# Transformer block, forward and backward: three quarters of dW2 computed behind the attention forward and summed in DRAM, the rest alternating with dW1

## The chip, the cores and the metric

The kernel runs on one core of a Trainium2 chip. It computes the output of a transformer block and all gradients in one launch. The metric is the device time of one execution in microseconds; less is better. The kernel before has a median of 2522.99 us in three runs (2513.47 to 2525.77).

## The reference

One sequence of 2048 tokens, width 512, 32 heads of 16, an MLP of width 1792, bf16. The six modulation vectors come from `silu(c) @ w_mod`. Cut to what matters here:

```python
def _B_ref(x, w1, b1, w2, b2):
    h = jnp.einsum('bsd,df->bsf', x, w1) + b1
    r = jnp.where(h > 0, h, 0)
    h = r * r
    return jnp.einsum('bsf,fd->bsd', h, w2) + b2
...
h = _layernorm(x) * (1 + ca) + sa
x = x + ga * _A_ref(h, A_wqkv, A_wo)        # attention over 32 heads
h = _layernorm(x) * (1 + cb) + sb
x = x + gb * _B_ref(h, B_w1, B_b1, B_w2, B_b2)
...
_out, _vjp = jax.vjp(_f, A_x, A_wqkv, A_wo, B_w1, B_b1, B_w2, B_b2, c, w_mod)
_grads = _vjp(grad_out)
```

The change concerns dW2, the gradient of `B_w2`: with a = r * r (1792 features by 2048 tokens) it is gb times a @ grad_out, a sum over all tokens. The sums dgb (dW2 times w2, over features) and the gradients of b2 and of the columns 3, 4 and 5 of w_mod hang on the same products. dW1 is the like sum of xhat and du over the tokens.

## The kernel before

**Stages.** Tokens come in four chunks of 512 (SC = 4), features in 14 blocks of 128 (FT), heads in 8 groups of 4 (NQ), keys in 16 blocks of 128 (ST). First come the projections together with the attention of chunk 0. Then `fwd_rest` runs the attention of chunks 1 to 3: 3 x 8 x 16 = 384 units, one per chunk, head group and key block. A unit is four score products (L503), two exps on ScalarE (L507) and sixteen small products of P and V (L482). `last_chunk` then does the MLP and its backward for chunk 3 with no attention beside it, and the weight gradients dW1 (`gen_dw1`) and dW2 (`gen_dw2`) over all four chunks: the dW stage. The attention backward follows, then a last stage of projections.

**Background.** The MLP, forward and backward, of chunks 0 to 2 is written as generators (`gen_mlp`) that yield after each matrix product. Each unit of `fwd_rest` calls `bg.burst(3.0, self, most)`, which runs generators in the order in which they were added until its credit is spent, at most 4 products (5 or 2 in the first units of a group). Where it runs fewer, the unit adds products of the same size that nobody reads (L520, the filler). A tuple such as `("wait", 9)` is a marker: the background holds, and each unit takes 2 off. Other tuples mark places that the code can run up to (`until`).

**What a chunk's background holds.** When a chunk's last group is done, `take_o` copies its attention output, stores it to DRAM twice (`O_d`, L1264, in bf16 and L1266 in fp32) and `gen_mlp` starts. SyncE transposes the output (L1277) and grad_out (L1279) by DMA. Then follow the output projection and layernorm, fc1 with the relu (L1316, into `rT`), the backward through fc2 (L1326, into `auT`), the storing of both in DRAM (`duT_d`, `aT_d`), the backward through fc1 with a layernorm backward and the gradient of the attention output per 128 tokens (`gen_do`, which loads O_d by POOL at L1398), and fc2 for the four blocks of 128 tokens. Three of these four fc2 blocks come after the marker `fc2_2` in chunk 2, and `last_chunk` works them off at its start (`bg.take`, `bg.drain`).

**The dW stage.** `gen_dw1` takes one block of 128 features at a time: 64 products (L1096, 16 blocks of tokens by 4 of columns), one fp32 product that spreads db1 (`csb`, L1101), and per column tile three DVE operations (L1110, L1112, L1115) that form the block of dW1 and two sums. `gen_dw2` takes 16 products (L1151) per block, then two DVE operations (L1154, L1157) and a sum on POOL (L1158). Both need their features with tokens on partitions: `turned` loads per block 12 tiles by DMA transpose from DRAM (`tm_blk`, L1047) and, for the last chunk, four blocks at a time from SBUF (`tm_l`, L1051). dW2 begins when dW1's last block is under way. The columns 3 and 4 of the gradient of w_mod (L1170 to L1182) lie inside dW2, after its blocks 2 and 5. What the backward needs first is loaded in pieces between dW2's later blocks.

**What sets the order.** PE and SyncE work in the order of the program text; POOL, DVE and ACT in an order that the compiler's scheduler sets. The background has one PSUM bank (`pps`).

Of the kernel before, what the change touches and what calls it, by code (L numbers as in the profile page):

```python
# [112 lines left out]

class Pools:
# [12 lines left out]
class K:  # L127
# [32 lines left out]

    def build(self, ctx: ExitStack):
# [20 lines left out]
        self.WmT_d = self.dram("WmT_d", [DT, P, 3 * DT * P], BF16)  # L182
        self.dx1b_d = self.dram("dx1b_d", [512, D], BF16)
# [108 lines left out]
    def phase_fwd(self):  # L292
# [29 lines left out]
        QTm = [fw.tile([P, 512], BF16, name=f"QTm{j}") for j in range(4)]  # L322
# [139 lines left out]
    def fwd_rest(self, bg, KT, kp, pup, QTm, Vaug, O32):  # L462
# [33 lines left out]
        for n, (qc, g) in enumerate(groups):  # L496
            for kb in range(ST):
# [14 lines left out]
                done = 0 if qc == SC - 1 and f"fc2_{SC - 2}" in bg.seen else bg.burst(3.0, self, most)  # L512
# [348 lines left out]
    def last_chunk(self, bg, O_b, x0s, o32):  # L861
# [12 lines left out]
        tps = self.open_pool("tps", bufs=2, space=PSUM)  # L874
# [15 lines left out]
        g_tm = e0.tile([P, ST, D], BF16, name="g_tm")  # L890
        xh2 = e0.tile([P, ST, D], BF16, name="xh2")
        gt4, xh = g_tm[:, st0:, :], xh2[:, st0:, :]
        OT, gT = self.OT_l, self.gT_l
        nc.sync.dma_start(gt4, tm_v(io["grad_out"][0]))
        nc.sync.dma_start(xh2[:, :st0, :], self.xhat2_d.rearrange("(st p) d -> p st d", p=P)[:, :st0, :])
        nc.sync.dma_start(g_tm[:, :st0, :], io["grad_out"][0].rearrange("(st p) d -> p st d", p=P)[:, :st0, :])
# [56 lines left out]
        fill.add(self.gen_dw1(w1p, xh2, duT))  # L953
# [63 lines left out]
        fill.add(g2)  # L1017
# [9 lines left out]
        fill.until("dw1")  # L1027
        next(g2)
        self.open_bwd()
# [10 lines left out]
    def turned(self):  # L1040
# [4 lines left out]
        def get(pool, src, src_d, ft):  # L1045
            r = pool.tile([P, ST - 4, P], BF16, name="tm_blk", bufs=4)
            nc.sync.dma_start_transpose(r[:], src_d[ft, :, :(ST - 4) * P])  # L1047
            if ft % 4 == 0:
                n = min(4, FT - ft)
                t = pool.tile([P, 4, 4, P], BF16, name="tm_l", bufs=2)  # L1050
# [3 lines left out]
            return [r[:, st, :] for st in range(ST - 4)] + [lasts[-1][:, ft % 4, i, :] for i in range(4)]  # L1054
# [3 lines left out]
    def gen_dw1(self, sb, xh2, duT):  # L1058
# [6 lines left out]
        dsb_part = sb.tile([P, DT, FT], F32, name="dsb_part", bufs=1)  # L1065
        db1_row = sb.tile([P, 4 * P], BF16, name="db1_row", bufs=1)
# [18 lines left out]
        for ft in range(FT):  # L1085
# [4 lines left out]
            else:  # L1090
                yield ("dw1", 0)
            du, (w1_blk, diag) = dus[ft], blks[ft]
            g4 = self.dps.tile([P, DT, P], F32, name="dps")
            for kt in range(DT):
                for st in range(ST):
                    nc.tensor.matmul(g4[:, kt, :], lhsT=xh2[:, st, kt * P:(kt + 1) * P], rhs=du[st],  # L1096
                                     start=(st == 0), stop=(st == ST - 1))
                    if st % 4 == 3:
                        yield 1
            csb_ps = self.mps.tile([P, 512], F32, name="pps")  # L1100
# [6 lines left out]
            dw1 = sb.tile([P, DT, P], BF16, name="dw1")  # L1107
            for kt in range(DT):
# [5 lines left out]
                junk2 = sb.tile([P, P], BF16, name="junk", bufs=1)  # L1114
                nc.vector.scalar_tensor_tensor(junk2[:], csb[:], 1.0, w1_blk[:, kt, :], ALU.mult, ALU.mult,  # L1115
                                               accum_out=dsb_part[:, kt, ft:ft + 1])
            with nc.allow_non_contiguous_dma(reason="256B runs"):
                nc.gpsimd.dma_start(dw1_v[:, :, ft * P:(ft + 1) * P], dw1[:])
        for r in range(0, FT, 4):
# [3 lines left out]
        nc.vector.tensor_reduce(self.dsb_col[:], dsb_part[:], axis=AX.X, op=ALU.add)  # L1123

    def gen_dw2(self, sb, g_tm, aT, tb):
# [8 lines left out]
        def load(ft):  # L1134
            r = turned(tb, aT, self.aT_d, ft)
            w = sb.tile([P, D], BF16, name="w2_blk", bufs=3)
            nc.gpsimd.dma_start(w[:], io["B_w2"][ft * P:(ft + 1) * P, :])
            blks.append((r, w))

        mods = {2: (3, self.dsb_col), 5: (4, self.dcb_col)}  # L1140
# [4 lines left out]
        for ft in range(FT):  # L1145
            if ft + 3 < FT:
                load(ft + 3)
            a, w2_blk = blks[ft]
            pt = self.dps.tile([P, 512], F32, name="dps")
            for st in range(ST):  # L1150
                nc.tensor.matmul(pt[:], lhsT=a[st], rhs=g_tm[:, st, :], start=(st == 0), stop=(st == ST - 1))  # L1151
# [916 lines left out]
```

## Time and profile before

The profiled execution took 2527.3 us, with a span of 2525.3 us from the first instruction to the last.

| stage | from to, us | us |
|---|---|---|
| attention of chunks 1 to 3, with background | about 280 to 984 | 704 |
| start of the last chunk, up to fc1 | 984 to 1008.5 | 24.5 |
| MLP of the last chunk | 1008.5 to 1060 | 51.5 |
| dW1, with what is left of the last chunk | 1060 to 1124 | 64 |
| dW2 | 1124 to 1179.4 | 55.4 |
| backward and last stage | 1179.4 to the end | 1346 |

A row of a group of instructions reads: line, engine, operation, output and inputs, their shapes, the number of instructions, then busy microseconds and the mean of one in ns, then the idle time of the engine just before them and what ended it. A row of the timeline begins with start and length in microseconds. PE is the matrix engine, PEld its weight loads, DVE, ACT, POOL and SP the vector, scalar, GpSimd and sync engines. A row with SPq is the time that SP's queue spent issuing. Consecutive products overlap, so three or four of them have a combined length larger than the step from start to start.

### The profile page before, as it was taken

Reading aid. Unit: us, or ns where it says so; the run is one execution under the profiler, and the core shown is the slowest. Engines: PE = TensorE matmul, PEld = TensorE weight load, DVE = VectorE, ACT = ScalarE, POOL = GpSimd, SP = SyncE. Lnnn points to the kernel's source line nnn. Section 1 sums busy time; section 2 is a strip of 40 time slices with the busy share of each in tenths; the row PEclk is TensorE's granted clock in tenths of the full one; section 3 lists DMA queues with packets and bytes.
Section 4 is the critical chain, followed back from the end, with each engine's and each line's share of the span. In section 5 each row is a group of like instructions: output and inputs, shape, how many; then the busy total and the mean of one; then the engine's idle time right before and its main releaser. Section 6 shows DMA issues by size and latency. Waiting matters only on the chain.

```text
span 2525.3 us, 69141 instructions
## 1 busy us (share of the span) xinstructions
PE 2424.0 (96%) x26994; PEld 1032.7 (41%) x27199; DVE 1683.0 (67%) x3343; ACT 2283.0 (90%) x3757; POOL 715.7 (28%) x1265
## 2 busy tenths in 40 slices
PE   8999999999999999989999999999999999999988
PEld 4555444545554544573232333332333333333333
DVE  6222212322342333576999999999999999999857
ACT  7999999999999996533999999999999999999934
POOL 2344430120121021246222332322332323222323
PEclk9999999999999999999999999999999999999999
DMA  4689650451244054599999999999999999999997
GB/s 166 133 179 209 162 124 22 127 118 48 99 103 100 22 145 120 111 188 214 236 237 226 233 237 232 236 226 228 230 233 234 233 234 234 239 227 238 241 179 188
DMA packets 1291630, 454.19 MB, mean 180 GB/s; under 512 B 1235796, under 2 KB 1260246, under 8 KB 1291302
## 3 DMA queue, kind: packets, MB, share of 16 engines
q1 hardware_dynamic: 1252422, 344.68, 72.4%
q0 software_dynamic: 36800, 104.04, 14.1%
q8 instruction: 212, 3.47, 0.6%
q10 hardware_dynamic: 2080, 1.05, 0.2%
q14 instruction: 116, 0.95, 0.1%
HBM read 75.83 MB, written 64.49 MB: 56 GB/s over the span
## 4 chain that ended last, share of the span: by engine, by line
PE 40%; ACT 8%; DMA 8%; issue 2%; DVE 2%; POOL 0%; SPq 0%; DVEq 0%; ACTq 0%; POOLq 0%
PE st L1710 16%; PE acckv L1561 8%; ACT pu L1713 6%; PE accq L1586 5%; DMA dsT<-ds 4%; PE dps L1151 2%; PE dp L1624 2%; DMA keep<-ds 1%; DMA dqT<-dq_t 1%; ACT csq L1642 1%; PE st L1856 1%; DVE ds L1628 1%; PE dp L1761 1%; PE st L1667 1%; PE st L1574 1%
## 5 line engine op out<-in xcount | busy, mean ns | idle before, releaser
L1628 DVE TENSOR_TENSOR ds<-dp,pu 128x512 bf16<-128x512 f32 x1888 | 1166.8, 684 | 36.5 <-PE dp L1624 20.6
L1713 ACT ACTIVATE pu<-st 128x512 bf16<-128x512 f32 x2048 | 1073.6, 666 | 37.2 <-PE st L1710 21.3
L507 ACT ACTIVATE pu<-st 128x1024 bf16<-128x1024 f32 x768 | 704.9, 1127 | 6.0 <-PE st L503 5.6
L1624 PE MATMUL dp<-kvm,q 64*128 64x512 bf16 x1024 | 364.0, 383 | 2.1 <-DVE ds L1628 1.0
L1624 PE MATMUL dp<-kvm,dOTg 64*128 64x512 bf16 x1024 | 364.9, 384 | 1.0 <-DVE ds L1628 0.8
L1710 PE MATMUL st<-kvm,QTg 64*128 64x512 bf16 x1024 | 348.8, 382 | 6.0
L1710 PE MATMUL st<-kvm,q 64*128 64x512 bf16 x1024 | 347.9, 381 | 5.1 <-ACT pu L1713 0.2
L1643 POOL TENSOR_TENSOR ds<-csq,pu 128x512 bf16<-128x512 f32 x128 | 147.2, 1150 | 626.5 <-ACT csq L1642 547.4
L482 PEld LDWEIGHTS <-pu 128*128 128x128 bf16 x6144 | 216.5, 96 | 158.0 <-issue 83.2
L482 PE MATMUL accbank<-Vaug,pu 128*128 128x17 bf16 x6144 | 265.2, 172 | 10.1 <-ACT pu L507 7.4
L520 PE MATMUL st<-QTm,KTq 128*128 128x512 bf16 x670 | 202.7, 379 | 6.3 <-ACT pu L507 2.7
L413 ACT ACTIVATE pu<-st 128x1024 bf16<-128x1024 f32 x224 | 206.6, 1060 | 2.3 <-PE st L410 1.9
L503 PE MATMUL st<-QTm,KTq 32*128 32x512 bf16 x1536 | 171.9, 385 | 5.2 <-issue 1.0
L1561 PE MATMUL acckv<-ds,Qg 128*16 128x512 bf16 x1024 | 176.5, 383 | 0.2
L1561 PE MATMUL acckv<-pu,dOg 128*16 128x512 bf16 x1024 | 176.4, 383 | 0.0
L1561 PE MATMUL acckv<-ds,q 128*16 128x512 bf16 x1024 | 175.8, 382 | 0.0
L1561 PE MATMUL acckv<-pu,q 128*16 128x512 bf16 x1024 | 175.8, 382 | 0.0
L410 PE MATMUL st<-QTm,KTq 128*128 128x512 bf16 x435 | 130.0, 377 | 10.1 <-ACT pu L413 4.0
L1710 PEld LDWEIGHTS <-q 64*128 64x128 bf16 x1024 | 66.9, 94 | 162.9 <-issue 150.0
L1710 PEld LDWEIGHTS <-QTg 64*128 64x128 bf16 x1024 | 67.1, 94 | 161.5 <-issue 146.5
L347 PEld LDWEIGHTS <-pu 128*128 128x128 bf16 x2048 | 86.4, 96 | 59.6 <-issue 3.0
L1624 PEld LDWEIGHTS <-q 64*128 64x128 bf16 x1024 | 88.8, 93 | 51.3 <-issue 40.8
(399 smaller groups left out, 3365.7 us busy)
## 6 DMA issues: line engine op xcount, KB each, us to landing
KTq<-KTq_d POOLq DMA_DIRECT2D x24, 512.0 KB, 3.8
duT_d<-auT POOLq DMA_DIRECT2D x3, 1792.0 KB, 7.3
aT_d<-rT POOLq DMA_DIRECT2D x3, 1792.0 KB, 11.9
KTq_d<-KTq SPq DMA_DIRECT2D x32, 128.0 KB, 2.2
QTq_d<-ev_fm SPq DMA_DIRECT2D x32, 128.0 KB, 4.4
ktm_d<-ev_tm POOLq DMA_DIRECT2D x32, 128.0 KB, 2.6
VTq_d<-vT POOLq DMA_DIRECT2D x4, 1024.0 KB, 6.1
dx<-dx_d SPq DMA_DIRECT2D x16, 256.0 KB, 4.6
```

What stands on the lines that cost most here:

```text
L410: nc.tensor.matmul(stt[:, a, :], lhsT=KT[:, kb * P:(kb + 1) * P], rhs=QTm[2 * jp + a][:], start=True, stop=True)
L413: nc.scalar.activation(pu[:], stt[:], ACT.Exp, scale=self.scale)
L482: nc.tensor.matmul(acc[:, j, sub, :], lhsT=pus[half][:, a, sub * P:(sub + 1) * P], rhs=Vaug[:, kb, 4 * g + j, :], start=(kb == 0 and j == ...
L503: nc.tensor.matmul(tiles[h // 2][:, h % 2, :], lhsT=KT[r, kb * P:(kb + 1) * P], rhs=QTm[g % 2][r, :], start=True, stop=True)
L507: nc.scalar.activation(pu[:], t[:], ACT.Exp, scale=self.scale)
L520: nc.tensor.matmul(tiles[0][:, 0, :], lhsT=KT[:, 0:P], rhs=QTm[g % 2][:], start=True, stop=True)
L1561: nc.tensor.matmul(acckv[r:r + DH, :], lhsT=T[n][:, ib, col:col + DH], rhs=src[:, a, :], start=(ib == 0), stop=(ib == ST - 1))
L1624: nc.tensor.matmul(dp[:], lhsT=T["dOT"][rd, ib * P:(ib + 1) * P], rhs=masked["VT"][a][rd, 512 * c:512 * (c + 1)], start=True, stop=True)
L1628: nc.vector.tensor_tensor(dsg[:, i, a], dp[:], pu[:, a, :], ALU.mult)
L1643: nc.gpsimd.tensor_tensor(dsg[:, i, 1], f[:], pu[:, 1, :], ALU.mult)
L1710: nc.tensor.matmul(stt[:], lhsT=T["QT"][rs, q], rhs=masked["KT"][a][rs, c0:c0 + 512], start=True, stop=True)
L1713: nc.scalar.activation(pu[:, a, :], stt[:], ACT.Exp, scale=self.scale)
```

## The change

**dW2 of chunks 0 to 2 as background.** A new generator, `gen_early`, computes per block of 128 features the four products of one chunk (180 in all, with a 15th block of ones for db2) and leaves an fp32 sum of 128 x 512 in DRAM, `dw2p_d`. Chunk 0 stores its products; chunks 1 and 2 load the sum so far, add and store. The transposed features are read back from `aT_d` by DMA, two blocks ahead, into three buffers; the sums have four, in the space of `auT`. The blocks of chunks 0 and 1 are computed in the background of the next chunk, 0 to 6 ahead of the output projection and 7 to 14 in place of a marker; chunk 2's between its own fc2 blocks 1 and 2. Only fc2's block 3 is left behind the marker `fc2_2`. The burst's rate goes from 3.0 to 4.0.

**dW stage.** `gen_dw2` computes the last chunk only, four products per block instead of 16, and adds the loaded fp32 sum (three DVE operations per block). `weave` alternates its blocks with those of dW1 from dW1's fourth block on. From then on dW1's sum over csb times w1 is no longer taken by DVE: four PE transposes, an ACT copy and a product (`add_rows`) do it. The columns 3 and 4 of w_mod's gradient come after dW1's last block.

```diff
-                done = 0 if ... else bg.burst(3.0, self, most)
+                done = 0 if ... else bg.burst(4.0, self, most)
...
-        yield ("wait", 9 if sc else 14)
+        if sc:
+            self.open_early(sc - 1)
+            yield ("wait", 12)
+            yield from self.gen_early(sc - 1, 0, FT // 2)
+        else:
+            yield ("wait", 14)
...
-            yield ("wait", 11)
+            yield from self.gen_early(sc - 1, FT // 2, FT + 1)
...
+        if sc == SC - 2:
+            self.open_early(sc)
         yield from fc2(0)
         yield from self.gen_do(sc, *todo.pop(0))
+        yield from fc2(1)
+        if sc == SC - 2:
+            yield from self.gen_early(sc, 0, FT + 1)
+        yield from fc2(2)
         yield (f"fc2_{sc}", 0)
-        for k in range(1, 4):
-            yield from fc2(k)
+        yield from fc2(3)
...
+    def load_early(self, c, ft):
+        if ft < self.FT:
+            nc.sync.dma_start_transpose(self.dw_blk[ft % 3], self.aT_d[ft, :, 512 * c:512 * (c + 1)])
+        if c:
+            nc.sync.dma_start(self.dw_sum[ft % 4], self.dw2p_d[ft])
...
+    def gen_early(self, c, a, b):
+        for ft in range(a, b):
+            if ft + 2 <= FT:
+                self.load_early(c, ft + 2)
+            pt = self.mps.tile([P, 512], F32, name="pps")
+            for st in range(4):
+                lhs = self.dw_blk[ft % 3][:, st, :] if ft < FT else self.ones_b[:]
+                self.mm(pt[:], lhsT=lhs, rhs=self.dw_op[:, st, :], start=(st == 0), stop=(st == 3))
+                yield 1
+            s = self.dw_sum[ft % 4]
+            if c:
+                nc.vector.tensor_tensor(s, pt[:], s, ALU.add)
+            else:
+                nc.vector.tensor_copy(s, pt[:])
+            nc.gpsimd.dma_start(self.dw2p_d[ft], s)
```

```diff
         next(g2)
+        fill.gens = [weave(g1, g2)]
+        fill.until("bwd")
         self.open_bwd()
...
+            if ft >= F0:
+                ...
+                for kt in range(DT):
+                    nc.tensor.transpose(tp[:, kt, :], w1_blk[:, kt, :], self.ident[:])
+                turnedw[ft] = sb.tile([P, D], BF16, name="w1T", bufs=2)
+                nc.scalar.copy(turnedw[ft][:], tp[:].rearrange("p a b -> p (a b)"))
+                if ft > F0:
+                    add_rows(ft - 1)
...
-            for st in range(ST):
-                nc.tensor.matmul(pt[:], lhsT=a[st], rhs=g_tm[:, st, :], start=(st == 0), stop=(st == ST - 1))
+            for st in range(4):
+                nc.tensor.matmul(pt[:], lhsT=a[st], rhs=g_tm[:, st, :], start=(st == 0), stop=(st == 3))
                 yield 1
-            dw2 = sb.tile([P, D], BF16, name="dw2")
-            nc.vector.tensor_tensor(dw2[:], pt[:], self.mod_row(5), ALU.mult)
...
+                nc.vector.tensor_tensor(part[:], pt[:], part[:], ALU.add)
+                dw2 = sb.tile([P, D], BF16, name="dw2")
+                nc.vector.tensor_tensor(dw2[:], part[:], self.mod_row(5), ALU.mult)
+                nc.gpsimd.dma_start(io["out_6"][ft * P:(ft + 1) * P, :], dw2[:])
+                nc.vector.tensor_tensor(part[:], part[:], w2_blk[:], ALU.mult)
+                nc.gpsimd.tensor_tensor(dgb[:], dgb[:], part[:], ALU.add)
```

**SP, opening of the last chunk's attention.** First the kernel before, then the kernel with the change. `fT` holds the transposed attention output and grad_out, `QTm_143`, `QTm_144` and `auT` the early operands.

```order
192 L1434 DMA_TRANSPOSE dOTq<-dOpad_4895 128x8x128
193 L1277 DMA_TRANSPOSE fT<-O_b 128x16x128
194 L1279 DMA_TRANSPOSE fT<-in_grad_out_dram 128x4x512
195 L1302 DMA_TRANSPOSE fT<-xh_14265 128x16x128
196 L1343 DMA dx_d<-dx_16110 128x512
```

```order
207 L1560 DMA_TRANSPOSE dOTq<-dOpad_4896 128x8x128
208 L1355 DMA_TRANSPOSE fT<-O_b 128x16x128
209 L1357 DMA_TRANSPOSE fT<-in_grad_out_dram 128x4x512
210 L1467 DMA auT<-in_grad_out_dram 128x4x512
211 L1475 DMA_TRANSPOSE QTm_143<-aT_d 128x4x128
212 L1477 DMA auT<-dw2p_d 128x512
213 L1475 DMA_TRANSPOSE QTm_144<-aT_d 128x4x128
214 L1477 DMA auT<-dw2p_d 128x512
215 L1475 DMA_TRANSPOSE auT<-aT_d 128x4x128
216 L1477 DMA auT<-dw2p_d 128x512
```

The early operands, and a sum per block, come into SP's order behind the two large transposes.

**ACT, from the last blocks of dW1 to the backward.** Before, then with the change. `csb` and `t` belong to dW1, `O_20016` and `O_20348` are scratch of the modulation columns (diagonal, then the row), and `pu<-st` is the backward's first exp.

```order
117 L1170 ACTIVATE O_20016<-ident_f,dcb_col 128x128
118 L1170 ACTIVATE O_20016<-ident_f,dsb_col 128x128 x4
119 L1170 ACTIVATE O_20016<-ident_f,dcb_col 128x128 x3
120 L1175 COPY O_20016<-dps 128x512
121 L1179 ACTIVATE auT<-O_20016,scT 128x512 x4
122 L1175 COPY O_20016<-dps 128x512
123 L1179 ACTIVATE auT<-O_20016,scT 128x512 x4
124 L1713 ACTIVATE pu<-st 128x512 x6
```

```order
130 L1154 ACTIVATE t_20295<-csb,modT 128x128 x4
131 L1167 COPY dsb_rows<-tp 32x512
132 L1208 ACTIVATE O_20348<-ident_f,dcb_col 128x128 x4
133 L1217 COPY O_20348<-dps 128x512
134 L1221 ACTIVATE auT<-O_20348,scT 128x512 x4
135 L1217 COPY O_20348<-dps 128x512
136 L1839 ACTIVATE pu<-st 128x512
137 L1221 ACTIVATE auT<-O_20348,scT 128x512
138 L1839 ACTIVATE pu<-st 128x512 x2
139 L1221 ACTIVATE auT<-O_20348,scT 128x512 x3
140 L1839 ACTIVATE pu<-st 128x512 x3
```

The column work now stands directly between dW1's last block and the first exps, and its last four operations lie among these; before, all of dW2 after its block 5 lay between.

More of the change, by code (lines that the diff above doesn't have):

```diff
@@ L111, in drain, with weave @@
             pass
+def weave(*gens):
+    gens = list(gens)
+    while gens:
+        for g in list(gens):
+            while True:
+                r = next(g, None)
+                if r is None:
+                    gens.remove(g)
+                    break
+                if r == ("step", 0):
+                    break
+                yield r
 class Pools:
@@ L1134, in load @@
         def load(ft):
[L1135 to L1140, printed above, removed]
+            r, w = [self.ones_b[:]] * 4, None
+            if ft < FT:
+                r = turned(sb, aT, None, ft)
+                w = sb.tile([P, D], BF16, name="w2_blk", bufs=3)
+                nc.gpsimd.dma_start(w[:], io["B_w2"][ft * P:(ft + 1) * P, :])
@@ new lines, in load, with mod_a @@
+            part = sb.tile([P, D], F32, name="part2", bufs=3)
+            nc.sync.dma_start(part[:], self.dw2p_d[ft])
+            blks.append((r, w, part))
+        nw = DT * D
+        mods = []
+        def mod_a(j):
+            i = len(mods)
+            if not mods:
+                self.mod_low = self.ra.tile([P, FT * 512], BF16, name="auT")
+                self.mod_hi = self.ra.tile([P, 4, D], F32, name="O32")
+            low, hi = self.mod_low, self.mod_hi
+            dg, dm = hi[:, 2 * i, :], hi[:, 2 * i + 1, :]
+            wm = low[:, i * nw:(i + 1) * nw].rearrange("p (kt d) -> p kt d", d=D)
+            nc.gpsimd.dma_start(wm, io["w_mod"].rearrange("(kt p) n -> p kt n", p=P)[:, :, j * D:(j + 1) * D])
+            col = self.dcb_col if j == 4 else self.dsb_col
+            for kt in range(DT):
+                nc.scalar.activation(dg[:, kt * P:(kt + 1) * P], self.ident_f[:], ACT.Copy, scale=col[:, kt:kt + 1])
+            mods.append((j, dg, dm, wm))
@@ new lines, in mod_b @@
+        def mod_b(j, dg, dm, wm):
+            low = self.mod_low
+            pt = self.dps.tile([P, 512], F32, name="dps")
+            nc.tensor.matmul(pt[:], lhsT=self.ones_f[:], rhs=dg, start=True, stop=(j == 4))
+            if j == 3:
+                nc.tensor.matmul(pt[:], lhsT=self.ones_f[0:32, :], rhs=self.dsb_rows[:], start=False, stop=True)
+            nc.scalar.copy(dm, pt[:])
+            for kt in range(DT):
+                c = 2 * nw + kt * D
+                o = low[:, c:c + D]
+                nc.scalar.activation(o, dm, ACT.Copy, scale=self.scT[:, kt:kt + 1])
+                nc.gpsimd.dma_start(io["out_9"][kt * P:(kt + 1) * P, j * D:(j + 1) * D], o)
+                c = 2 * nw + DT * D
+                nc.vector.scalar_tensor_tensor(low[:, c:c + D], dm, 1.0, wm[:, kt], ALU.mult, ALU.mult,
+                                               accum_out=self.dc_part[:, kt, j:j + 1])
@@ L1141, in gen_dw2, with mod_step @@
+        left, due = [4, 3], []
+        def mod_step():
+            ready = due[:]
+            due.clear()
+            if self.dw1_done and left:
+                mod_a(left.pop(0))
+                due.append(mods[-1])
+            for m in ready:
+                mod_b(*m)
         load(0)
```

144 lines of the change are left out of this document (78 added, 66 removed).

## The prediction, made before the changed kernel ran

> **What bounds the kernel now.** I began with the page's busy shares, then cut the span into the stages that the change touches and read each engine's busy time there.
>
> ```profile
> PE 2424.0 (96%) x26994; PEld 1032.7 (41%) x27199; DVE 1683.0 (67%) x3343; ACT 2283.0 (90%) x3757; POOL 715.7 (28%) x1265
> ...
> L520 PE MATMUL st<-QTm,KTq 128*128 128x512 bf16 x670 | 202.7, 379 | 6.3 <-ACT pu L507 2.7
> ```
> ```profile
> 280.00:984.00 704.00, 678.55 (x9040) 349.80 (x9169) 209.02 (x513) 700.37 (x764) 122.53 (x182) 1.00 0.38 92
> 984.00:1008.50 24.50, 20.24 (x111) 9.78 (x113) 12.03 (x33) 5.67 (x9) 4.71 (x8) 0.93 0.54 188
> ...
> 1075.00:1124.00 49.00, 42.90 (x704) 42.45 (x702) 33.92 (x201) 18.17 (x62) 22.11 (x35) 0.97 1.06 176
> 1124.00:1179.40 55.40, 54.96 (x239) 24.57 (x243) 32.30 (x90) 10.54 (x24) 38.21 (x51) 0.97 1.14 245
> 1179.40:1250.00 70.60, 64.94 (x627) 18.74 (x630) 66.18 (x108) 66.06 (x130) 19.77 (x36) 1.00 1.10 209
> ```
>
> The columns behind the length are PE, PEld, DVE, ACT and POOL busy, the granted clock, the DMA share and GB/s. In the attention forward (280 to 984) ACT is busy 700.37 of 704.00 us: its exps set the pace. PE looks as full, but 202.7 us of its page total are the filler products of L520, which nobody reads. The dW stage (1060 to 1179) is the other way round: PE full, ACT nearly idle. Work that moves from the second place into fillers of the first is therefore free on PE, so long as it never makes PE, and through PE ACT, wait in the forward. The backward from 1179.4 on keeps ACT and DVE near full and starts when dW is done, so what dW loses the end loses too.
>
> **Forward: the swap itself.** One unit (a key block: four score products, two exps, sixteen products of P and V, fillers) repeats every 1.83 us, by the starts of its score products:
>
> ```profile
> 979.81 0.39 PE L503 MATMUL st<-QTm,KTq 32*128 32x512 bf16 x4
> ...
> 980.69 1.02 PE L520 MATMUL st<-QTm,KTq 128*128 128x512 bf16 x4
> 981.64 0.39 PE L503 MATMUL st<-QTm,KTq 32*128 32x512 bf16 x4
> ```
>
> The change adds 3 x (14 x 4 + 4) = 180 dW2 products of 512 columns and 2 x 15 = 30 of fc2 here, and the program has 760 - 550 = 210 fewer fillers. Four products take the filler's place in a unit, so PE's cost is 0. DVE gets 45 operations of about 0.69 us (the row of L1154 below is such a one) and is busy only 209 of 704 us: 0 as well.
>
> **Forward: waits added.** Two new ones can stop PE, and ACT with it.
>
> (a) At the opening of a query chunk the first dW2 products need their operands (a 512 KB load of grad_out and two transposes of aT_d blocks). In SP's order these stand behind the two transposes of the attention output and of grad_out:
>
> ```profile
> 752.37 0.76 POOL L1266 DMA_DIRECT2D O_d<-O  x1
> ...
> 769.60 0.57 POOL L1398 DMA_DIRECT2D o<-O_d  x1 [14.44 <-DMA O_d<-O]
> ```
> ```profile
> 752.29 11.22 SPq L1277 DMA_TRANSPOSE fT<-O_b  x1
> 763.56 8.22 SPq L1279 DMA_TRANSPOSE fT<-in_grad_out_dram  x1
> ```
> ```profile
> 529.11 3.66 SPq L1277 DMA_TRANSPOSE fT<-O_b  x1
> 532.82 4.00 SPq L1279 DMA_TRANSPOSE fT<-in_grad_out_dram  x1
> ```
>
> SP is free again at 771.8 for the last chunk and at 536.8 for the one before. The marker of 12 holds the background back for six units (a unit takes 2 off), and by the order the first dW2 products stand in the ninth unit of each of these chunks, 119 and 247 units ahead of the last one, which starts at 981.64: at 763.5 and 528.9, and 0.6 into the unit. In the kernel before fc2 of the previous chunk stands there, which needs none of these loads. The loads then need to be issued and to land: 768 to 776 and 537 to 541, a wait of 3 to 12 us at each; ACT's queue hides about 1. Bounds: 3 us for both together, if the queue runs ahead, and 22, if both are late. I take **13 us**, near the middle, since the rows show SP busy at the very time, but not how much of it is owed to the O_d stores that run beside it. ACT cannot win it back; it has 3.63 us of idle in 704.
>
> (b) From the second chunk on the sums run through DRAM in four buffers: add, store by POOL, load by SP four blocks on. Nearest rows of this size:
>
> ```profile
> o<-O_d POOLq DMA_DIRECT2D x12, 256.0 KB, 3.2
> dx_d<-dx SPq DMA_DIRECT2D x12, 256.0 KB, 2.3
> ```
> ```profile
> dx<-dx_d SPq DMA_DIRECT2D x16, 256.0 KB, 4.6
> ```
> ```profile
> L1154 DVE TENSOR_TENSOR dw<-dps,mod 128x512 bf16<-128x512 f32 x13 | 9.0, 690 | 18.8 <-PE dps L1151 11.1 <-DMA out_dram<-dw 4.8 <-PE dps L1173 3.0
> ```
>
> The last column of the first rows is us to landing. Lower end 0.69 + 0.57 (POOL's issue, as that of L1398 above) + 2.3 + 3.2 = 6.76 us for four blocks, 1.69 a block and below the unit's 1.83: nothing. Upper end with 4.6 twice: 10.46, 2.62 a block, 0.78 over the unit for the 2 x 11 blocks that reuse a buffer: 17 us. I take 3, close to the lower end, because the two lower rows are from the forward itself and the loaded 4.6 isn't.
> The Trainium skill, "DMA: Bandwidth & Descriptors", section "Anatomy of one DMA — SWDGE (gpsimd) path", fits a DMA by 2.0 us and its bytes at 436 GB/s; an estimate by that page is 2.6 us each way, a loop of 6.5 and a sum 3 us lower than mine. The trace's 2.3 and 3.2 us lie on both sides of it.
>
> **Start of the last chunk.** PE works off fc2 there between other steps:
>
> ```profile
> 1001.97 3.18 PE L158 MATMUL pps<-w,rT 128*128 128x512 bf16 x14 [0.78 <-DVE o L1362]
> ...
> 1008.51 1.25 PE L939 MATMUL pps<-fT,w 128*128 128x512 bf16 x5 [0.52 <-DVE fT L883]
> ```
> ```profile
> 999.34 0.81 ACT L924 ACTIVATE xh<-x_l,nmr,rstd 128x512 bf16<-128x512 f32 x1 [1.46 <-DVE nmr L923]
> ```
>
> Two of its three groups (30 products) go forward. fc1 (L939) then waits for the last xh, ready at 1000.15, rather than for the fc2 group that ends near 1005.4: it starts at about 1001.1, **-7.4 us**. That counts about 1 us from xh to fc1 for its transposes and their copies; more than 7.4 can't be had, since xh comes no earlier. At the lower end, 3.5 us, one group's 3.18 and its start still stand in the way; I take the upper, as the program has nothing of the two groups left there.
>
> **dW stage.** Rows for one woven pair, a dW1 block and a short dW2 block:
>
> ```profile
> L1103 ACT COPY csb<-pps x4: 265/265/265, 1065.7 to 1077.7; 128x128 f32<-128x128 f32 x4
> ```
> ```profile
> 1106.24 0.27 ACT L1103 COPY csb<-pps 128x128 f32<-128x128 f32 x1 [2.00 <-PE pps L1101]
> ...
> 1110.09 0.27 ACT L1103 COPY csb<-pps 128x128 f32<-128x128 f32 x1 [2.00 <-PE pps L1101]
> ```
> ```profile
> 1142.20 1.03 PE L1151 MATMUL dps<-g_tm,tm_l 128*128 128x512 bf16 x4
> 1143.06 1.02 PE L1173 MATMUL dps<-O,ones_f 128*128 128x512 f32 x2
> ```
> ```profile
> 1107.92 0.35 DVE L1110 SCALAR_TENSOR_TENSOR dw<-dps,opcbT,t 128x128 bf16<-128x128 f32 x1
> 1108.19 0.28 DVE L1115 SCALAR_TENSOR_TENSOR junk<-csb,w_blk 128x128 bf16<-128x128 f32 x1
> ...
> 1108.73 0.34 DVE L1110 SCALAR_TENSOR_TENSOR dw<-dps,opcbT,t 128x128 bf16<-128x128 f32 x1
> ```
>
> A dW1 block paces at 1110.09 - 1106.24 = 3.85 us; four dW2 products add 1143.06 - 1142.20 = 0.86; the four new transposes and the product of add_rows about 0.23 + 0.22 (one of the four 512-column products above is 0.86/4). PE's pair: **5.16 us**. DVE needs 4 x (0.81 - 0.28) + 3 x 0.69 = 4.2, so PE paces. The third dW1 block ends by the rows of csb near 1073.6; 7.4 earlier is 1066.2; then one dW2 block, ten pairs and the last dW1 block: T = 1066.2 + 0.86 + 51.6 + 3.85 = 1122.5. PE has no 3.7 us wait for DVE here, as DVE has 0.28 less per tile.
>
> The queue of SP is the cover in question:
>
> ```profile
> q1 hardware_dynamic: 23916, 6.01, 65.6%
> ```
> ```profile
> q1 hardware_dynamic: 28820, 8.77, 83.1%
> ```
> ```profile
> 1120.82 10.34 SPq L1047 DMA_TRANSPOSE tm_blk<-aT_d  x4
> ```
>
> These are SP's transfers in 1060 to 1124 and 1124 to 1179.4: 42.0 + 46.0 = 88 us. Fourteen tm_blk transposes go, 2.6 each, -36; fifteen fp32 loads of 256 KB come, at 88 us for 14.8 MB 1.6 each, +23 (that mean holds transposes, so hardly more). Up to 75 us must fit in about 72. I charge **+3 us**; bounds 0 and 8.
>
> **Tail before the backward.** The modulation columns now follow the last dW1 block instead of lying inside dW2:
>
> ```profile
> 1106.81 1.28 ACT L1109 ACTIVATE t<-csb,modT 128x128 f32<-128x128 f32 x4
> ...
> 1133.90 1.26 ACT L1170 ACTIVATE O<-ident_f,dsb_col 128x128 f32<-128x128 f32 x4
> ...
> 1144.12 0.58 ACT L1175 COPY O<-dps 128x512 f32<-128x512 f32 x1 [8.09 <-PE dps L1173]
> 1144.74 2.56 ACT L1179 ACTIVATE auT<-O,scT 128x512 bf16<-128x512 f32 x4
> ...
> 1179.83 3.14 ACT L1713 ACTIVATE pu<-st 128x512 bf16<-128x512 f32 x6 [21.31 <-PE st L1710]
> ```
> ```profile
> L1182 DVE SCALAR_TENSOR_TENSOR auT<-O,auT 128x512 bf16<-128x512 f32 x8 | 8.0, 997 | 0.4 <-ACT O L1175 0.2
> ```
>
> There they cost only the 1.02 us on PE, once each. Now they stand in the way. From T: copy of csb and the four t on ACT (0.27 + 1.28, and some 0.3 for db1's row between them), DVE's last tile and a dW2 operation (0.53 + 0.69), four diagonal columns (1.26), the product (1.02), and 0.7 for the sum over blocks and the steps from engine to engine, which no row gives singly: 6.1 us. Then ACT's 0.58 + 2.56 + 0.58 and another 2.56 among the first exps: 12.4. ACT belongs to the backward from 1134.9, against 1179.8 before: **-45 us** with the 7.4 included. On DVE the eight products of L1182 (8.0 us) start near T + 6.7 and end near T + 14.7; for that lateness I take off 2: **-43**. Bounds: -48, if the columns run wholly beside the first exps, and -40, if the backward waits for both columns in full (another 3 us).
>
> **Sum.** -43 + 3 (SP queue) + 13 (openings) + 3 (loop) = -24 on the profiled execution of 2527.3: **2503 us**. That execution is 4.3 above the median, inside the runs' spread.
>
> **Rivals.**
> *All hidden.* SP runs ahead at the openings and the loop stays under the unit: 2527.3 - 43 = 2484. For it: the loop's lower rows; against it: SP busy to 771.8.
> *dW becomes SP's.* The stage doesn't shorten as said: the queue's 75 us and the openings at 22 leave -43 + 8 + 22 + 3 = -10, 2517.
> *The DRAM loop paces the forward.* Place: chunks with a sum to load. It adds 22 x (L/4 - 1.83) us for a loop of L; with the openings at 22 and 3 for SP, the gain of 43 is gone from L = 10.6. At L = 13 it costs 31: 2540, slower. For it: SP is in order, and a load waiting for its store holds the next transposes; against: 2.3 and 3.2 us.
> *Clock.* Where PE idles, 984 to 1008.5, the clock is 0.93, so 1.7 us lost; two opening waits and the tail would add 2 to 5: 2506. The Trainium skill, "TensorE: Matmul & The Clock Gate", section "Part 1: The HAM clock gate (the "warmup" mystery)", has the clock at half after an idle window of about 3.4 us; that 0.93 agrees.
>
> **How the numbers follow.** Forecast 0.42, clock 0.08, all hidden 0.27, SP's queue 0.15, DRAM loop 0.08. Range 2479 to 2530: from all hidden with the tail's bound of -48, past 2517 to the loop at its bound of 17 us on top of the full openings (2527.3 - 43 + 3 + 22 + 17 = 2526, and some). About 0.5% (12.6 us) is what a measurement can tell from no change. Faster than that: all hidden, forecast and clock save 0.1 of their upper part, and a third of the queue case: 0.27 + 0.40 + 0.05 = 0.72. Same 0.22, slower 0.06.
>
> **What would show it.** Right: ACT in the forward waits for PE once after each chunk opening, 3 to 12 us, with PE waiting for a DMA to auT or QTm; csb copies 5.2 us apart; first pu exp of the backward near 1147 (1131 and the 16 us of forward waits). Wrong: a forward no longer than before (then all hidden), csb copies over 5.5 us apart with PE waiting for tm_blk or part (SP's queue), or PE's early products waiting for DVE, and DVE for dw2p, block after block (the loop).

## The result, and the profile after

The changed kernel takes 2546.31 us (median of 5 runs, 2539.51 to 2556.3), the kernel before 2521.26 beside it (5 runs): ratio 1.0101 with the interval 1.0067 to 1.0135. It is slower by about 25 us where 24 us less were forecast; the forecast's range ended at 2530. The profiled execution took 2540.45 us.

By stage, from the first and last records of a line (exps of the forward, fc1, dW1's products, csb, exps of the backward). The backward's start is taken where its 40th exp ends, less 40 times the mean step of 0.592 us before, since the first exps after the change are scattered:

| stretch, us | before | after | difference | forecast |
|---|---|---|---|---|
| to the forward's last exp | 983.1 | 1024.1 | +41.0 | +16 |
| last exp to fc1 | 25.4 | 20.7 | -4.7 | -7.4 |
| fc1 to dW1's first product | 51.6 | 54.1 | +2.5 | 0 |
| dW1's first product to the backward's start | 120.0 | 107.6 | -12.4 | -32.6 |
| sum at the backward's start | 1180.1 | 1206.5 | +26.4 | -24 |

The rest, about 1332 against 1345 us, agrees less well. Its code is the same, and over all kernels of this document it took 1332 to 1348 us; 12 us of the difference lie behind the backward's last exp, where the profiles show 120 to 133 us. Why is open. The medians confirm the +25.

The waits of PE up to 1250 us, in us in total, times and the longest:

```profile
PE pps L173 <- DMA QTm<-aT_d: 22.2, 8, 5.0
PE dps L1131 <- DMA tm_blk<-duT_d: 6.7, 4, 3.0
...
PE pps L173 <- DVE auT L1492: 5.3, 3, 1.9
```

None of these existed before. Busy time by stretch, columns as in the prediction:

```profile
273.60:1025.00 751.40, 703.66 (x9220) 368.30 (x9218) 243.50 (x564) 707.39 (x768) 153.06 (x234) 0.97 0.48 125
1025.00:1044.80 19.80, 15.41 (x84) 7.56 (x84) 10.51 (x31) 5.46 (x9) 3.59 (x6) 0.78 0.42 139
1044.80:1098.90 54.10, 54.10 (x257) 24.15 (x258) 28.71 (x86) 30.15 (x53) 10.66 (x17) 0.95 0.36 78
1098.90:1188.60 89.70, 78.94 (x1049) 67.11 (x1048) 60.30 (x238) 34.25 (x102) 53.98 (x77) 0.94 1.10 227
```

In the forward ACT is busy 707 of 751 us: it now has 44 us of idle, where it had 3.6 of 704. In the dW stage PE is busy 79 of 90 us, so it waits there too. Before, ACT ran from 499.5 to 900.4 without a wait that the timeline shows:

```profile
499.50 400.89 ACT L507 ACTIVATE pu<-st 128x1024 bf16<-128x1024 f32 x437
```

With the change it stood still in the forward at these places, with the time that it stood in brackets:

```profile
529.47 1.94 ACT L525 ACTIVATE pu<-st 128x1024 bf16<-128x1024 f32 x2 [4.04 <-PE st L521]
...
558.31 1.94 ACT L525 ACTIVATE pu<-st 128x1024 bf16<-128x1024 f32 x2 [3.37 <-PE st L521]
566.23 1.94 ACT L525 ACTIVATE pu<-st 128x1024 bf16<-128x1024 f32 x2 [5.98 <-PE st L521]
...
780.79 1.94 ACT L525 ACTIVATE pu<-st 128x1024 bf16<-128x1024 f32 x2 [4.46 <-PE st L521]
...
821.75 1.94 ACT L525 ACTIVATE pu<-st 128x1024 bf16<-128x1024 f32 x2 [6.03 <-PE st L521]
...
996.83 1.94 ACT L525 ACTIVATE pu<-st 128x1024 bf16<-128x1024 f32 x2 [3.72 <-PE st L521]
```

Summed with the smaller ones between (over 0.5 us): 4.0 and 6.7 at the two openings, 10.7 and 12.6 some 20 to 45 us later, 8.2 in chunk 2's own run: 42.2, all of the forward's +41.0. The second pair is the largest and the forecast hasn't it. What stands there, on PE and on SP (the first of the pair):

```profile
555.60 1.86 PE L173 MATMUL pps<-auT 128*128 128x512 bf16 x4 [2.67 <-DVE auT L1494]
563.49 1.89 PE L173 MATMUL pps<-auT,QTm 128*128 128x512 bf16 x4 [4.96 <-DMA QTm<-aT_d]
```
```profile
538.50 1.24 SPq L1475 DMA_TRANSPOSE auT<-aT_d  x1
555.02 2.17 SPq L1385 DMA_TRANSPOSE fT<-xh  x1
557.25 4.55 SPq L1475 DMA_TRANSPOSE QTm<-aT_d  x2
```

After its layernorm the chunk goes on at once with early block 7. Its copy on DVE stands behind the layernorm, and the operand of block 9 stands in SP's order behind the transpose of xh, which waits for the layernorm until 555.02. Before, a marker of 11 let the forward run on with fillers just here. At the two places behind the layernorm PE itself waits 10.0 us for operands and 7.8 us for DVE. Behind the waits it is slower, which can make up the rest of the 23.3: the granted clock is at half for 13.7 us from 554.9 on:

```profile
554.90:568.60 13.70, 8.04 (x64) 3.47 (x63) 2.42 (x5) 3.92 (x5) 2.45 (x4) 0.50 0.67 172
```

### The profile page after: what moved, and what is told of

Same layout as the page of the kernel before. It is cut to its first block, busy times and chain, and to the rows that moved or that the text cites. A ratio compares the mean times of both kernels' runs of the same rounds, so it can differ in the third digit from the quotient of the medians.

```text
span 2538.7 us, 69299 instructions
## 1 busy us (share of the span) xinstructions
PE 2418.5 (95%) x27046; PEld 1035.1 (41%) x27046; DVE 1710.4 (67%) x3322; ACT 2291.8 (90%) x3769; POOL 743.0 (29%) x1310
## 4 chain that ended last, share of the span: by engine, by line
PE 40%; ACT 7%; DMA 7%; issue 2%; DVE 2%; POOL 0%; SPq 0%; DVEq 0%; ACTq 0%; POOLq 0%
PE st L1836 16%; PE acckv L1687 8%; ACT pu L1839 6%; DMA dsT<-ds 5%; PE accq L1712 5%; PE dp L1750 2%; PE dp L1887 2%; PE st L1982 1%; DVE ds L1754 1%; PE dps L1131 1%; ACT csq L1768 1%; PE st L1793 1%; PE st L1700 1%; PE pps L956 1%; PE gps L2022 1%
## 5 line engine op out<-in xcount | busy, mean ns | idle before, releaser
L1839 ACT ACTIVATE pu<-st 128x512 bf16<-128x512 f32 x2048 | 1072.9, 662 | 16.8 <-PE dp L1750 12.4
L500 PEld LDWEIGHTS <-pu 128*128 128x128 bf16 x6144 | 221.1, 96 | 161.7 <-issue 91.0
L538 PE MATMUL st<-QTm,KTq 128*128 128x512 bf16 x550 | 146.0, 378 | 2.2 <-ACT pu L525 2.2
L428 PE MATMUL st<-QTm,KTq 128*128 128x512 bf16 x448 | 132.7, 377 | 6.1 <-ACT pu L431 4.0
L1836 PEld LDWEIGHTS <-q 64*128 64x128 bf16 x1024 | 67.1, 94 | 165.3 <-issue 152.3
L1712 PE MATMUL accq<-dsT,keep 128*32 128x256 bf16 x1632 | 105.5, 278 | 6.1 <-DMA dsT<-ds 6.0
L1750 PEld LDWEIGHTS <-dOTg 64*128 64x128 bf16 x1024 | 88.5, 93 | 54.7 <-issue 45.0
```

The source lines that it names most:

```text
L500: nc.tensor.matmul(acc[:, j, sub, :], lhsT=pus[half][:, a, sub * P:(sub + 1) * P], rhs=Vaug[:, kb, 4 * g + j, :], start=(kb == 0 and j == ...
L538: nc.tensor.matmul(tiles[0][:, 0, :], lhsT=KT[:, 0:P], rhs=QTm[g % 2][:], start=True, stop=True)
L1712: nc.tensor.matmul(accq[r:r + 32, o:o + 256], lhsT=T["K"][:, 4 * c + sub, col:col + 32], rhs=v[:, r // 32 % 2 * 2:r // 32 % 2 * 2 + 2, 4 * ...
L1750: nc.tensor.matmul(dp[:], lhsT=T["dOT"][rd, ib * P:(ib + 1) * P], rhs=masked["VT"][a][rd, 512 * c:512 * (c + 1)], start=True, stop=True)
L1836: nc.tensor.matmul(stt[:], lhsT=T["QT"][rs, q], rhs=masked["KT"][a][rs, c0:c0 + 512], start=True, stop=True)
L1839: nc.scalar.activation(pu[:, a, :], stt[:], ACT.Exp, scale=self.scale)
```

## The experiments

"Forward" is the last exp's start, "stretch" is dW1's first product to the last csb: 1024.1 and 89.7 us in the change. Each kernel was run once unless an interval is given, and single runs differ where nothing was changed. In the eight kernels with the change's forward (the change, e3, e6 to e9, e13, e14) it ends at 1022.6 to 1032.8, with stalls of 4.0 to 5.4 and 6.3 to 8.3 us at the openings, 9.1 to 11.6 and 11.4 to 14.6 behind the layernorm, and 5.7 to 10.7 in chunk 2's own run. In the five with the change's dW stage (the change, e1, e2, e5, e7) the stretch is 88.1 to 99.4. Only what lies outside these spans counts below. In time the single runs of e1 to e3, e6 to e9, e13 and e14 took 2546 to 2565 us: none is a gain over the change's 2540 to 2556.

**e1_first: operands ahead of the opening's transposes.**
```diff
+        if sc:
+            self.open_early(sc - 1)
         OT = mk.tile([P, 4, DT, P], BF16, name="fT", bufs=2)
```


> Only the place of the early operands in SP's order changes: their first loads (the 512 KB of grad_out, two blocks, two sums) are issued ahead of the two large transposes at a chunk's opening. Theory A (the forward lost its time because the operands of the early products stand late in SP's order) expects the stalls of ACT at the two openings, 4.0 and 4.5 us plus the small ones behind them, to go: the forward some 8 to 12 us shorter, the stalls after the layernorm (10 and 11 us) unchanged. Theory B (the DRAM round trip of the sums paces the early products) expects no change beyond 3 us. Theory C (DMA bandwidth beside the O_d stores) expects the same stall, moved to the output projection.

Measured: the stalls at the openings 0.6 and 4.2 (of it 1.3 at the first products) in place of 4.0 and 6.7, those after the layernorm 11.1 and 11.5, unchanged, forward 1018.5. The openings' stalls lie below their spans, so theory A holds in kind for the openings; the gain, 5.6 us, is under its 8 to 12.

**e2_nosum: no loads of the sums in the forward.**
```diff
-        if c:
-            nc.sync.dma_start(self.dw_sum[ft % 4], self.dw2p_d[ft])
...
-                nc.vector.tensor_tensor(s, pt[:], s, ALU.add)
+            nc.vector.tensor_copy(s, pt[:])
```


> The early sums aren't loaded nor added: each chunk copies its own product and stores it, so dW2, db2 and the column sum over dW2 hold only what chunks 2 and 3 add. Theory B (DRAM round trip) expects the forward back near the length of the kernel before, at least 25 of its 42 us gone. Theory A (place in SP's order) expects both openings and both stalls after the layernorm to stay and only the third run of early blocks, chunk 2's own (8.5 us), and part of the second (up to 6) to go: 8 to 15 us in all.

Measured: chunk 2's own run 0 in place of 8.2, openings 5.3 and 6.5, after the layernorm 10.2 and 11.0; forward 1016.8. The loads of the sums cost their 8 us, and only there. The forward's gain, 7.3 us, is at the edge of theory A's 8 to 15, and B as the main cause falls.

**e5_mark: e1, and the marker back behind the layernorm.**
```diff
-            yield ("wait", 12)
+            yield ("wait", 6)
...
+            yield ("wait", 11)
             yield from self.gen_early(sc - 1, FT // 2, FT + 1)
```


> The order of the first experiment (operands ahead of the opening's two large transposes), the opening's marker cut from 12 to 6, and a marker of 11 (six units) put back between the layernorm and the second run of early blocks. Theory A (place in SP's and DVE's order) expects the stalls after the layernorm, 10 to 13 us in each of two chunks, to go down to under 2 each, while chunk 2's own run keeps its 8: the forward ends some 25 to 35 us sooner than in the change, and the time is near that of the kernel before (2515 to 2525). If instead each early run loses its time to the DMA engines' load, the stalls move six units later and the forward stays within 8 us of the change.

Measured: stalls after the layernorm 0 and 0.8, chunk 2's run 6.1, forward 1000.7, 23.4 us sooner (under the 25 to 35 of theory A), time 2524.46 (before 2529.06 beside it). Where the change stalls twice from 558 to 568, ACT now runs through:

```profile
532.53 53.45 ACT L525 ACTIVATE pu<-st 128x1024 bf16<-128x1024 f32 x58 [0.84 <-PE st L521]
```

The openings are back at 6.3 and 6.7: the marker was cut to 6, and PE waits 4.7 and 5.1 us for the third block, which still stood behind the large transposes. Theory A is shown for the stalls behind the layernorm: nothing but places in the order has changed, and the stalls didn't move six units on. What SP's order and what DVE's had in them isn't separated.

**e4_dwonly: no early products at all.** The dW stage and the earlier fc2 stay; fp32 rows of another tensor are added.

> The forward computes no early products (so dW2, db2 and the column sum over dW2 lack the first three chunks and add unrelated numbers of the same size loaded from another tensor); the dW stage and the earlier fc2 are those of the change. If the prediction's ledger of the later stages is right in kind, the forward has the length of the kernel before within 2 us and the time lies 15 to 30 us under the kernel before. If the early fc2 or the burst's rate of 4.0 costs the forward too, it is longer than before by over 5 us.

Measured: forward 982.9, last exp to fc1 16.8, time 2497.83 against 2522.27 beside it. Without early work the later stages give 24 us (21.8 at the backward's start). The stretch is 87.5, so the dW stage falls short with the forward out of the way too.

**e3_nopart, e6_runs: what fills the dW stage.** e3 drops the loads of the sums in the dW stage, e6 reads w1 and writes dW1 in 1 KB runs.

> The dW stage doesn't load the fp32 sums of chunks 0 to 2 (a copy of the last chunk's product takes the place of the add), so dW2, db2 and the column sum over dW2 lack the first three chunks. If SP's queue with its sum loads holds back the transposes of dW1 (a load waits for one of three buffers and everything behind it waits too), the 14 csb copies stand in 66 to 72 us in place of 83.5, with the three gaps of 9 to 10 us gone, and the time falls by 12 to 17 us. If the DMA engines' load or DVE is the limit, it falls by under 6.

> In the dW stage the blocks of w1 and of dW1 are read and written as contiguous pieces of 1 KB in place of 256-byte runs, so they lie in the wrong places and dW1's two column sums use wrong weights; instructions and bytes stay. Theory D (the dW stage is paced by the DMA engines, which are busy for over 90 percent of it, and small pieces weigh most) expects dW1's first product to the last csb to take 70 to 80 us in place of 89, with the gaps over 6 us gone. If SP's order alone is the cause, it stays at 85 to 95.

Measured: stretch 88.1 and 86.9; the one at the lower edge of the unchanged stage's span, the other 1.2 us under it, and neither near the 66 to 80 that the theories asked for. In e3 the steps between csb are 5.4 us on average for eight blocks, and then one of 14.8 comes, where PE waits 8.5 us for w1:

```profile
PE tp L1140 <- DMA w_blk<-in_B_w_dram: 8.5, 1, 8.5
```

POOL, which issues that load, had waited 12.5 us to load w_mod into the space of auT.

**e8_wm, e9_part: blocked heads of queues.** e8 loads w_mod into other space; e9 moves the loads of the sums to POOL as well.

> Only the dW stage differs from the change: the two loads of w_mod's columns go into the space of O32, free before the woven blocks, in place of the space of auT, where POOL waits 10 us for the last transpose out of it with dW1's loads and stores queued behind. Theory E (blocked instructions at the head of the in-order queues of POOL and SP make the gaps of the dW stage) expects one of the three gaps of 9 to 10 us in the steps between csb products to go: first product of dW1 to the last csb 89.7 us down to 83 to 86. Theory D (DMA engines full) expects 87 to 91.

> The edit before, and the loads of the fp32 sums issued by POOL in place of SP, so that a load which waits for its buffer no longer holds the transposes of dW1. Theory E expects the steps between csb products at 5.4 to 6 us but for the first of the woven ones and one more: first product of dW1 to the last csb 76 to 82 us. Theory D expects 86 or more.

Measured: 97.0 and 95.0, inside the span of the unchanged stage, so E's gain didn't come. But these kernels don't test E cleanly: the same edit puts the diagonals of the columns into the space of auT, and there ACT waits 5.6 us in e8 and 9.0 in e9, in POOL's place. In e9 the steps are 5.3 to 5.4 in six of eleven, but the first is 18.4, as PE waits 10.4 us for the first transposes of rT.

**e10_all, e11_best, e12_spmod: all of it together.** e10 has e9's dW stage and e5's forward with markers 9 and 11, six sum buffers, and sums four blocks ahead. e11 asks for three operand blocks ahead of the large transposes, and for rT and w_mod at other times; in e12 w_mod's load goes to SP.

> Both edits of the dW stage, and a forward with the early operands ahead of the opening's two transposes, markers of 9 and 11 before the two early runs, six sum buffers in place of four, and sums loaded four blocks ahead. Theories A (order) and B (the DRAM loop, for chunk 2's own run only) expect the forward's last exp within 12 us of the kernel before (983): 985 to 995, with the stalls of chunk 2's own run down from 8 to under 3. With the dW stage at 76 to 82 the time is 20 to 30 us under the kernel before: 2493 to 2503. If the queues only pass the wait on to the DMA engines, 2510 to 2520.

> The kernel of the last experiment with three edits: at an opening all three operand blocks are requested ahead of the two large transposes and later ones right after the block that frees the buffer; the first transposes of the last chunk's dW2 operand are issued some 20 us sooner, ahead of the end of the last chunk's work; the columns of w_mod are loaded during blocks 5 and 7 of the weave. Theory E expects the first woven step, 18 us, to fall under 9, so that the first product of dW1 to the last csb takes 76 to 82 us in place of 91; theory A expects the opening stalls (1.1 and 6.8 us) under 2 each. In all 12 to 18 us less than the last experiment: 2513 to 2519, 0.2 to 0.5 percent under the kernel before. If the stage keeps 88 us or more, its gaps aren't made by the queues' order but by the transfers themselves, and the time stays near 2528.

> The kernel of the last experiment, but w_mod's columns are loaded by SP behind all transposes, into the old place, and the diagonals are back in the space of O32: no instruction of ACT or POOL waits for the last transpose out of auT any more (21 us on ACT in the last experiment, PE behind it). Theory E expects the step of 21.3 us between csb products to go back to about 6, so the first product of dW1 to the last csb takes 78 to 85 us in place of 100 and the time falls by 10 to 16 us, to 2508 to 2525. If transfers make the gaps, another gap of 8 to 15 us takes its place.

Measured: ratios 1.0036 (1.0005 to 1.0068), 1.0050 (1.0029 to 1.0072), 1.0045 (1.0019 to 1.0071): from 1.0 percent slower to about 0.4, none faster than before. Forwards 997.3, 992.5, 997.0. In chunk 2's own run 6.7, 5.5 and 6.6 us of stalls are left, where e10 expected under 3, and at e11's second opening 4.7, where it expected under 2. Stretches 92.0, 99.8, 101.9. The new place of the diagonals holds ACT, and PE behind it, until the last transpose out of auT, for 8.2 us in e10 and far longer in e11:

```profile
1137.82 1.28 ACT L1207 ACTIVATE auT<-ident_f,dsb_col 128x128 f32<-128x128 f32 x4 [21.32 <-DMA tm_l<-auT]
```

In e12, without it, two steps of 15 us took its place, with PE waiting for tm_blk (10.3) and tm_l (5.2). That is what e12 expected if transfers make the gaps, and the clearest miss of theory E, which expected 78 to 85.

**e13_half, e14_late: less to transfer.** e13 reuses every second transposed block of du; e14 loads the backward's first group after the weave.

> In the dW stage every second block of dW1 reuses the transposed du of the block before it, so dW1's odd blocks are wrong and seven of its fourteen large transposes (384 KB each) aren't issued; all else is the change. Theory D (SP's transposes and the transfers beside them pace the stage, whoever waits) expects the first product of dW1 to the last csb to fall from 89.7 us, and from the 87 to 102 of all variants so far, to 72 to 80, with the steps between csb products at 5.4 to 6.5. Theory E (blocked instructions at the heads of queues) expects 84 or more, since every wait for a buffer is still there.

> The loads of the backward's first group are issued by SP after the last woven block in place of between the blocks; all else is the change. Theory D expects the dW1 stretch 4 to 9 us shorter than 89.7, and the backward's start later by about that or more, since some 2.5 MB then stand between. If the loads between the blocks cost the stage nothing, the stretch stays at 87 to 92.

Measured: stretch 82.6 in e13, between the two theories. It holds one wait at its start (first csb after 9.8 us in place of 6.2). The eleven woven steps sum to 67.0, against 76.1 in the change (74.5 to 85.7 in the five kernels with its dW stage) and 59.4 for eleven steps of 5.4: with half of dW1's transposes 9.1 of 16.7 us of gaps are gone, in one run of each. e14: stretch 85.9, 3.8 less, under D's 4 to 9. The first exp comes 18.5 us behind the last csb in place of 9.8, but counted at the 40th exp the backward's start lies 18.4 behind it in place of 17.9. So some 3 us are left, no more than single runs differ by.

**e7_tail: no columns 3 and 4.**
```diff
-                nc.scalar.activation(o, dm, ACT.Copy, scale=self.scT[:, kt:kt + 1])
...
+            nc.vector.memset(self.dc_part[:, :, j:j + 1], 0.0)
```


> The columns 3 and 4 of the gradient of w_mod are left out: their scaling on ACT, their stores and the eight DVE products behind them (their share of the gradient of c is zero). The tail's theory (what stands between the last dW1 block and the backward's steady pace is ACT's 5.1 us and DVE's 8 to 9 us of this work) expects the backward's 100th exp 8 to 11 us sooner, counted from the last csb product, which is 80 us in the change. If the tail is the wait for the loads of the backward's first group, it moves by under 3.

The diagonals, the product and its copy stay. Measured, from the last csb: the 100th exp at 78.5 in place of 78.6 us, but with one wait of PE of 5.2 us for dsT in between, where the change's profile has 2.5 in two. At the 40th exp the backward's start lies 13.1 us behind the last csb in place of 17.9 (17.9 to 19.7 in the fourteen kernels that have the columns behind dW1): the columns cost 4.8 there.

**e15_fc2: the kernel before, with the earlier fc2 alone.**
```diff
-        yield (f"fc2_{sc}", 0)
-        for k in range(1, 4):
-            yield from fc2(k)
+        yield from fc2(1)
+        yield from fc2(2)
+        yield (f"fc2_{sc}", 0)
+        yield from fc2(3)
```


> The kernel before with one part of the change alone: two of the three fc2 groups of chunk 2 run in fillers of the forward's last units, and one is left for the start of the last chunk. The prediction's term of 7.4 us expects the last chunk's fc1 to start 7 to 9 us sooner counted from the forward's last exp (25.4 us in the kernel before), the forward no longer by over 1, and the time 6 to 9 us (0.25 to 0.35 percent) under the kernel before. The rival, that the start of the last chunk hides fc2 behind its own chain, expects under 2.

Measured: last exp to fc1 16.8 in place of 25.4, forward 708.9 us from first to last exp (708.0), ratio 0.9965 (0.9946 to 0.9985), 2514.58 against 2522.73. It is the fastest kernel here that leaves nothing out, 0.35 percent under the kernel before. The start of fc1:

```profile
1001.43 1.90 PE L939 MATMUL pps<-fT,w 128*128 128x512 bf16 x8 [0.52 <-DVE fT L883]
```

## Why the prediction was wrong

**The swap on PE** was right. The forwards of e4 and e15, with the 30 products of fc2 and no early ones, are as long as before. For the 180 early products there is the sum of ACT's stalls: at 42.2 us it is all of the 41.0 that the forward lost, so a unit without a stall is no longer than before.

**"Two new ones can stop PE"** was the step that failed. There are three. The openings were sized well (13 forecast, 4.0 + 6.7 measured), at the first partly by luck: SP was free at 522.3, not at 536.8, and PE's early products came sooner too. Behind the layernorm the change replaces the marker of 11 by work, and I gave that edit no price, though the order showed the transpose of xh in the middle of the early operands: 10.7 + 12.6 = 23.3 us. e1 and e2 leave them as they are (22.6 and 21.2), and e5 takes them away with a marker.

**The DRAM loop** was under-sized: 3 us forecast, 8.2 measured in chunk 2's own run, and 0 without the loads (e2). Its rows, and the waits of SP and PE from 950 to 1030:

```profile
dw2p_d<-auT POOLq DMA_DIRECT2D x45, 256.0 KB, 3.7
auT<-dw2p_d SPq DMA_DIRECT2D x30, 256.0 KB, 4.1
```
```profile
SPq L1477 <- DMA dw2p_d<-auT: 10.0, 5, 4.5
```
```profile
PE pps L173 <- DMA QTm<-aT_d: 5.2, 4, 3.3
```

0.69 + 0.57 + 3.7 + 4.1 = 9.1 us for four blocks, 2.27 a block against 1.83. Over the 11 blocks of chunk 2 that reuse a buffer that makes 4.8 us, not 8.2. PE waits for the transposed operands, which stand in SP's order behind loads that wait for their stores: the rival's "a load waiting for its store holds the next transposes", at a smaller size. With six buffers and loads four blocks ahead (e10 to e12) 5.5 to 6.7 us are left, so more buffers don't cure it. The rows that I took, 2.3 and 3.2 us, were a store by SP and a load by POOL, and here it is the other way round. Why these take 3.7 and 4.1 is open. The sums' own traffic alone isn't it, as the stores take 3.5 in e2 too, where no sum is loaded in the forward.

**The start of the last chunk**: -7.4 forecast, -8.6 alone (e15), so "more than 7.4 can't be had" was wrong by 1.2: the chain up to xh became shorter too. In the change it is -4.7, with PE's clock there at 0.78. The other runs bear the clock out: in the seven kernels where it is 1.00 up to dW1 and the early fc2 is in (e2, e4, e5, e10 to e12, e15), this stretch takes 16.8 us (17.9 in e2) and the MLP 51.6; in the four where it is 0.78 or 0.79 and then 0.95 (the change, e3, e7, e14), 20.7 and 54.1 or 54.2:

```profile
1001.80:1017.50 15.70, 12.47 (x81) 6.12 (x83) 10.42 (x31) 5.37 (x8) 3.58 (x6) 1.00 0.54 176
1017.50:1069.20 51.70, 51.35 (x253) 23.58 (x258) 28.32 (x86) 29.95 (x53) 10.60 (x17) 1.00 0.41 82
```

These rows are e5's. The clock rival thus came, with 3.9 + 2.5 = 6.4 us in these two stretches, where it forecast 2 to 5 in all.

**The dW stage** was forecast as PE's, with 3 us charged to SP. The pair is 5.4 us where nothing waits, 5.16 forecast, 2.6 us over eleven. The miss is the gaps: 16.7 us beyond eleven such steps in the change, most of them at three places, where PE waits for transposes:

```profile
1115.01 1.89 PE L1248 MATMUL dps<-g_tm,tm_l 128*128 128x512 bf16 x4 [2.51 <-DMA tm_l<-rT]
```
```profile
1138.00 0.49 PE L1146 MATMUL pps<-diag,ones_f 128*128 128x128 f32 x2
1141.90 1.45 PE L1131 MATMUL dps<-tm_blk,xh 128*128 128x128 bf16 x12 [2.55 <-DMA tm_blk<-duT_d]
1147.75 0.49 PE L1146 MATMUL pps<-diag,ones_f 128*128 128x128 f32 x2
```
```profile
1175.84 1.28 PE L1131 MATMUL dps<-tm_blk,xh 128*128 128x128 bf16 x12 [3.00 <-DMA tm_blk<-duT_d]
```
```profile
1114.60:1118.00 3.40, 2.99 (x17) 1.89 (x18) 1.07 (x3) 0.00 (x0) 0.38 (x1) 0.51 1.28 325
1142.00:1145.40 3.40, 3.40 (x34) 3.40 (x34) 1.49 (x3) 0.00 (x0) 3.40 (x6) 0.51 1.05 256
1176.10:1179.50 3.40, 3.40 (x36) 3.40 (x34) 0.91 (x2) 0.00 (x0) 2.38 (x4) 0.50 1.63 323
```

The step around the second takes 9.75 us. PE's waits of over 0.25 us in the stretch sum to 10.6 us, and the clock, at half for 3.4 us at each of the three places, takes 1.7 each: 15.7 of the 16.7. On SP the loads of sums stand in the way:

```profile
1115.46 7.49 SPq L1191 DMA_DIRECT2D part<-dw2p_d  x2
```

Two that wait for a buffer hold SP for 7.5 us at once, and all of them together 15.6 us. The term that failed is "75 us must fit in about 72", charged with 3 us: a queue that full has no slack, so whatever blocks its head for a moment can become PE's gap. That is how I read the trace, and it is not shown: without these loads (e3) or with them on POOL (e9) the gaps are as long, at other places. All variants with dW1 whole move the gaps (stretches of 85.9 to 101.9) but don't remove them. For the transposes' share e13 speaks: there SP waits 38 us for buffers of sums, and yet the stretch is the shortest, so a wait at the head costs little where the queue has less to do. What makes the other half, 7.6 us, stays open, and so does whether an order of SP's queue exists that avoids the gaps. Gaps, pair and tail, less the 3 us charged, make 19.8 of the 20.2 us that this stage misses.

**The tail**: 12.4 and 2 for lateness forecast, 17.9 measured; e7 puts 4.8 on the columns. The rest lies between the last dW2 operations on DVE and a PE at reduced clock, and wasn't separated:

```profile
1198.30:1208.00 9.70, 3.52 (x15) 0.93 (x15) 9.60 (x22) 6.03 (x12) 7.58 (x11) 0.59 0.46 166
1208.00:1218.00 10.00, 9.09 (x54) 1.90 (x52) 8.88 (x16) 8.09 (x16) 1.77 (x3) 0.72 0.43 99
```

The rivals: none of them alone is what came. The slower case had its place right (the forward) and its main mechanism wrong: the loop gives a fifth of the forward's loss, the work in the marker's place behind the layernorm more than half. "dW becomes SP's" came in part, by the sign that was set for it: csb copies 6.9 us apart on average, with PE waiting for tm_blk.

## What to carry to other kernels

A marker or filler that hides a latency makes its price zero only as long as it stands: where a change puts work into it, look up in the order which queue carries that work's operands and what waits ahead of them in it. Price each in-order queue by what its head may wait for, not by its busy share alone, above all when the share is near full. Repeat a profile of an unchanged stage before a difference of a few microseconds is explained: here such stages differed by 10 us. And split a change with several parts before it is judged: one small part here was worth 8 us alone.

## What the runs showed of the hardware

Short waits cost more than themselves. After PE's gaps in the forward its clock was lower for a while: 0.97 over the whole forward and 0.78 in the 20 us behind it, where the kernel before had 1.00 and 0.93. In the dW stage waits of 2.5 to 3.0 us were enough for 3.4 us at half clock each, so a wait needn't last the 3.4 us that the prediction names. Nor is the 0.93 of the kernel before a sign of such a wait: it is 3.4 us at half from 984.5 on, and the longest wait of PE in the 4 us ahead of that is 0.6. And two of the changed kernels scatter more: e11's twelve runs go from 2518 to 2550 us, the kernel before's seventeen beside them from 2516 to 2530, and e10's ten from 2519 to 2551 against 2514 to 2532. e15's twelve don't (2507 to 2522), and why the two do is open.
